# q's and k's high parts kept once in DRAM, and each stack loaded in two transfers

## The chip, the core and the metric

The kernel runs on one core of a Trainium2 chip. A core has TensorE (PE: matmuls, with its weight loads shown apart as PEld), VectorE (DVE), ScalarE (ACT), GpSimd (POOL) and SyncE (SP), each with its own queue of instructions that it takes in order, and 16 DMA engines that move data between DRAM and the core's SBUF. The metric is the time of one execution in microseconds on the device, the median of several runs. The profile is of one further execution.

## The reference

The kernel computes, for x of 2048 rows and 512 columns, a gated mix of a sliding-window attention and a dense block. All matmuls are asked in float32.

```python
x = A_x
g = _sigmoid((x * gate_w).sum(-1, keepdims=True))
a = _A_ref(x, A_wqkv, A_wo)              # 32 heads of 16, window of 256 keys, softmax
b = _B_ref(x, B_w1, B_b1, B_w2, B_b2)    # 512 -> 1792, gelu, -> 512
return g * a + (1 - g) * b
```

In `_A_ref` the scores are q·k / 4 per head, masked to keys at most 255 places back, then softmax, then times v, then the output projection.

## The kernel before

**Precision by two parts.** A float32 number is kept as a high part (rounded to the matmul's type) and a low part (the rest). A product is then made of three: high·high, high·low and low·high. For the projections this is three matmuls (`mm3`, L101 to L103). For the scores, where a head has only 16 numbers, the three products are stacked along the contraction: 48 rows hold 16 dimensions times three parts. q's rows carry low, high, high, k's rows high, low, high.

**Stages.** First `qkv` computes q, k and v for four pieces of 512 rows (t = 0 to 3). `qk_out` splits each 128 x 512 result into its parts in the tile `qke` and stores them to the DRAM tiles `SQ[t]` and `SK[t]`, in which the rows of a head lie by dimension and part: 8 heads of a column group, 16 dimensions, 3 parts, 4 column groups, 512 positions. The store is two transfers: L327 writes both parts, L328 writes the high part once more as the third.

Then attention runs over 8 groups of four heads and, in each, over 16 blocks of 128 keys: 128 blocks in all. Four blocks, one piece of 512 positions, make what is called a stretch here; there are 32. Every block has four matmuls `sm` (L517), whose row maxima DVE takes, and, 12 blocks later in the order, four matmuls `st` (L563), of which ACT takes the exponential. The products with v (`pv`, L607) come once for each stretch, behind the first three st of the next. `sm` reads the stacks `qd` (48 rows for each of two heads, 96 together) and `kd`; `st` reads the stacks `qs` and `ks`, which have 4 more rows for the maxima. In between the matmuls of attention the dense block's matmuls (`u`, `y`) are dealt out, so that TensorE always has one at hand.

**The loads around the change.** All transfers are issued by SP, from one queue, in the order in which the program wrote them. `kd`, `qd` and `ks` have two slots, one for the stretch at work and one for the next. When the maxima of a stretch begin, `load_kd` (L486) and `load_qd` (through `put_pairs`, L478 for one head's rows, L473 and L475 for the other's) are written for the next one; when its st begin, `load_ks` (the same three lines of `put_pairs`). `load_qs` (L497, two transfers) is written about three stretches ahead. `kd` takes two transfers where the window reaches back into the piece before, otherwise one. In the same queue stand the loads of the dense block's weights (`raw_w`, L163, which ACT then copies at L171), its input (`mx`, L676), its partial sums (`YA`, `YB`, `ya`), v (`vbuf`, L503), and the normalization of the attention: numerator and denominator out (`ND`, L635), the denominator back (`den`, L645, whose reciprocal DVE takes at L649), its reciprocal out and back, broadcast (`RD` L652, `rb` L657), the product out (`OT`, L664). The program places the readers of such a load a fixed time behind it in their engines' queues; an engine that gets there early waits.

**What an SP instruction waits for.** Beside its data's semaphores every transfer carries one of eight completion semaphores, DMAHW0 to DMAHW7, called lanes here. They are dealt out in turn, and a transfer is issued only when the one before it on its lane has landed. So at most eight transfers are on their way.

Of the kernel before, what the change touches and what calls it, by code (L numbers as in the profile page):

```python
# [9 lines left out]
F32 = mybir.dt.float32  # L10
# [7 lines left out]
S, D, F, H, DH, W = 2048, 512, 1792, 32, 16, 256  # L18
T = 512
NT = S // T  # L20
NB = T // 128
NC = D // 128
# [10 lines left out]
def gated_mix(ctx: ExitStack, tc: tile.TileContext, x, wqkv, wo, w1, b1, w2, b2, gate_w, out):  # L33
    nc = tc.nc
    x = x[0]
# [4 lines left out]
    dr = ctx.enter_context(tc.tile_pool(name="dr", bufs=1, space=DRAM))  # L40
# [4 lines left out]
    def f32(ap):  # L45
        return ap.bitcast(F32)
# [2 lines left out]
    nc.gpsimd.memset(idle, 0.0)  # L49


    SQ = [dr.tile([H // NC, 16, 3, NC, T], F32, name=f"SQ{t}") for t in range(NT)]
    SK = [dr.tile([H // NC, 16, 3, NC, T], F32, name=f"SK{t}") for t in range(NT)]
    SV = [dr.tile([128, NB, 2, H // 2 * 17], F32, name=f"SV{t}") for t in range(NT)]
    XT = [dr.tile([NC, 128, 2, T], F32, name=f"XT{t}") for t in range(NT)]
    OT = [dr.tile([NC, 128, T], F32, name=f"OT{t}") for t in range(NT)]
# [20 lines left out]
    for r in (0, 64):  # L77
        for e in (0, 1):
            v = cut[r:r + 64, e]
# [7 lines left out]
    for s in (0, 1):  # L87
        for k in (0, 1):
            v = own[64 * s:64 * s + 4].rearrange("r (p s) -> r s p", s=2)[:, s]
# [18 lines left out]
    def after(ns, fn, *args):  # L108
        now[1] += 1
        heapq.heappush(todo, (now[0] + ns, now[1], fn, args))  # L110

    def step_todo():
        due, _, fn, args = heapq.heappop(todo)
        keep, now[0] = now[0], due
        fn(*args)
        now[0] = max(keep, due)
# [6 lines left out]
    def need(*keys):  # L123
        for key in keys:
            while key not in done:
                step_todo()
# [88 lines left out]
    qs = cp.tile([128, 2, S], F32R, name="qs")  # L215
    ks = cp.tile([128, 2, 2, 2 * T], F32R, name="ks")
    qd = cp.tile([128, 2, 2, 2 * T], F32R, name="qd")
    kd = cp.tile([128, 2, 2, W + T], F32R, name="kd")
# [93 lines left out]
    def qk_out(t, j, p):  # L312

        dst, i = (SQ[t], j) if j < NC else (SK[t], j - NC)
        e = sb.tile([128, 2, T], F32R, tag="h", bufs=7, name=f"qke{t}_{j}")

        h = 1 if j < NC else 0

        def hi():
            nc.scalar.activation(e[:, h], p, AF.Copy)  # L320

        def lo():
            nc.vector.tensor_sub(e[:, 1 - h], p, f32(e[:, h]))  # L323

        def store():
            to = dst[:, :, :, i].rearrange("h d s c -> (h d) s c")
            nc.sync.dma_start(to[:, 0:2], f32(e))  # L327
            nc.sync.dma_start(to[:, 2], f32(e[:, h]))  # L328
            done.add(("qk", t, j))
        after(100, hi), after(700, lo), after(700 + HOLDQ, store)  # L330

# [36 lines left out]
    def qkv(t):  # L368
# [30 lines left out]
        for n, (kind, j) in enumerate(pieces):  # L399
# [18 lines left out]
            if t == 2 and n in (1, 2):  # L418
                load_kd(0, n - 1)
            if t == 2 and n in (8, 9):  # L420
                load_ks(0, n - 8)
# [22 lines left out]
    def slot(g_, c):  # L444
        return (g_ * NT + c) % 2

    def heads(st, g_):

        return st[2 * (g_ % 4):2 * (g_ % 4) + 2, :, :, 2 * (g_ // 4):2 * (g_ // 4) + 2]

    def ready(t, g_, k):
        need(*[("qk", t, k * NC + 2 * (g_ // 4) + a) for a in range(2)])

    def part(st, g_, s):

        return heads(st, g_)[s].rearrange("d u a c -> (d u) (a c)")

    def load_ks(g_, c):


        ready(c, g_, 1)
        n = 2 * NB
        put_pairs([f32(ks[64 * s + 4:64 * s + 52, slot(g_, c)]) for s in range(2)], SK[c], g_)

    def put_pairs(to, st, g_):

        n = 2 * NB
        for s in range(2):
            v = to[s].rearrange("r a x -> r (a x)")
            src = part(st, g_, s)  # L470
            if s:
                mid = v[:, 192:192 + 256 * (n - 1)].rearrange("r (n x) -> r n x", x=256)[:, :, 0:128]
                nc.sync.dma_start(mid, src[:, 64:64 + 128 * (n - 1)].rearrange("r (n x) -> r n x", x=128))  # L473
                ends = v.rearrange("r (n j) -> r n j", j=64)[:, 0:4 * n:4 * n - 1]
                nc.sync.dma_start(ends, src.rearrange("r (n j) -> r n j", j=64)[:, 0:2 * n:2 * n - 1])  # L475
            else:
                v = v.rearrange("r (n x) -> r n x", x=256)[:, :, 64:192]
                nc.sync.dma_start(v, src.rearrange("r (n x) -> r n x", x=128))  # L478

    def load_kd(g_, c):  # L480
        for t in range(max(c - 1, 0), c + 1):
            ready(t, g_, 1)
            k0 = 0 if t == c else T - W
            at = W if t == c else 0
            src = heads(SK[t], g_)[:, :, :, :, k0:].rearrange("s d u a c -> (s d u) a c")
            nc.sync.dma_start(f32(kd[0:96, slot(g_, c), :, at:at + T - k0]), src)  # L486

    def load_qd(g_, c):
        ready(c, g_, 0)
        put_pairs([f32(qd[48 * s:48 * s + 48, slot(g_, c)]) for s in range(2)], SQ[c], g_)  # L490

    def load_qs(g_, c):
        ready(c, g_, 0)
        need(("v", NT - 2, NB - 1))
        for s in range(2):
            v = f32(qs[64 * s + 4:64 * s + 52, :, c * T:(c + 1) * T])
            nc.sync.dma_start(v, part(SQ[c], g_, s).rearrange("r (a c) -> r a c", a=2))  # L497

    def att_load_v(g_, c):
        need(*[("v", c, b) for b in range(NB)])  # L500
# [171 lines left out]
    def load_x(t, name):  # L672
        xt = sb.tile([128, NC, 2, T], F32R, tag="xt", bufs=1, name=f"{name}{t}")

        def part(c):
            nc.sync.dma_start(f32(xt[:, c]), XT[t][c])  # L676
            if c == NC - 1:
                done.add(name)
        for c in range(NC):
            after(MXAT * c, part, c)  # L680
        xts[t] = xt
# [235 lines left out]
    for c in (0, 1):  # L917
        load_qd(0, c)
    fill(AHEAD)
    for u in range(-LEAD, NU):  # L920
        m = u + LEAD
        gm, bm = divmod(m, NKB)
        step = STEP if u >= 0 else STEP0
        for i in range(4):
            if i == 1 and m % NB == 0 and NB <= m < NU - NB:
                load_kd(*divmod(m // NB + 1, NT)), load_qd(*divmod(m // NB + 1, NT))
            for op in ORDER:
                if op == "s" and u >= 0:
                    att_exp(u // NKB, u % NKB, i)
                if op == "m" and m < NU:  # L930
                    att_max(gm, bm, i ^ XOR)
                if op == "p" and i == PVAT and u >= 1:
                    att_pvs(u - 1)
                if op == "f":
                    fill(step / 4 / ORDER.count("f"))
        if m < NU and bm % RB == RB - 1:
            after(900, att_rows, gm, bm // RB)
        if m % NB == QAT % NB and QAT <= m < QAT + NKB:
            load_qs(0, (m - QAT) // NB)
        if u % NB == 0 and NB <= u < NU - NB:  # L940
            load_ks(*divmod(u // NB + 1, NT))
        if u % NB == 2 and NB < u < NU - 3 * NB:
            load_qs(*divmod(u // NB + 3, NT))
        if u % NB == 0 and u >= 0:
            att_load_v(*divmod(u // NB, NT))
        if u - NU + NKB in (9, 11, 13):
            load_y((u % NKB - 9) // 2)
# [60 lines left out]
```

## Time and profile before

| | |
|---|---|
| median of 3 runs | 758.23 us (756.12 to 759.04) |
| the profiled execution | 755.15 us, its span 753.4 us |
| granted TensorE clock | 0.998 |
| DMA | 172.10 MB, mean 228 GB/s |
| HBM | read 108.53 MB, written 62.39 MB |
| chain that ended last | PE 83%, DMA 6%, DVE 4%, ACT 3% |

The profile names engines as above; SPq is SP's queue of DMA issues, L12 is line 12 of the kernel, and `out<-in` are the program's own names of the tiles. Times are in microseconds from the start of the span where nothing else is said. The time of an SPq row is that of the issue, not of the transfer. A wait row tells who waited, for whom, the sum, how often, and the longest.

### The profile page before, as it was taken

To read this page: it belongs to the slowest core of one execution; us is meant where nothing else is said; L and a number is where in the kernel's file an instruction comes from. 1 tells how busy PE (TensorE), PEld (TensorE's weight loads), DVE (VectorE), ACT (ScalarE), POOL (GpSimd) and SP (SyncE) were. 2 spreads that over 40 slices of the span, in tenths; PEclk is the share of its full clock that TensorE was granted. 3 is DMA by queue.
4 is the path that set the end of the run, shared out by engine and by line. 5 is a ranking of instruction groups with operands and counts; after the bars stand their busy time and mean duration, and the time that the engine had idled before them with its cause. 6 is when DMAs were issued, how large, how long until landed. Compare 5 with 4: busy or idle time off the path is not lost.

```text
span 753.4 us, 17968 instructions
## 1 busy us (share of the span) xinstructions
PE 737.4 (98%) x6129; PEld 608.8 (81%) x6129; DVE 519.2 (69%) x1567; ACT 431.4 (57%) x972; POOL 373.0 (50%) x846
## 2 busy tenths in 40 slices
PE   8999999989999999999999999999999999999998
PEld 7888888877888888888887877888888888878787
DVE  4522325779767866986798699768867886784562
ACT  4434532348646844864696478547845864785541
POOL 4200000338866765785677567757865875630000
PEclk9999999999999999999999999999999999999999
DMA  9879899998999699799986899998799999638683
GB/s 296 335 242 398 276 390 262 245 324 172 265 233 203 139 229 220 180 212 227 205 186 158 219 218 205 263 248 160 174 233 246 180 215 273 152 88 260 211 271 123
DMA packets 179258, 172.10 MB, mean 228 GB/s; under 512 B 56672, under 2 KB 122976, under 8 KB 179168
## 3 DMA queue, kind: packets, MB, share of 16 engines
q1 hardware_dynamic: 179168, 170.97, 87.6%
q8 instruction: 48, 0.79, 0.5%
q14 instruction: 42, 0.34, 0.2%
HBM read 108.53 MB, written 62.39 MB: 227 GB/s over the span
## 4 chain that ended last, share of the span: by engine, by line
PE 83%; DMA 6%; DVE 4%; ACT 3%; issue 2%; SPq 1%; POOL 1%; DVEq 0%; ACTq 0%; POOLq 0%
PE sm L517 9%; PE st L563 8%; PE pv_sm L607 7%; PE y L101 7%; PE y L103 6%; PE y L102 6%; PE u L101 5%; PE u L103 5%; PE u L102 5%; PE qk L103 4%; PE qk L101 4%; PE qk L102 4%; PE v L103 2%; PE v L102 2%; PE v L101 2%
## 5 line engine op out<-in xcount | busy, mean ns | idle before, releaser
L522 DVE CUSTOM_DVE_ANT_0 jm<-sm,mask 128x320 bf16<-128x320 f32 (+4 forms) x512 | 237.8, 464 | 81.1 <-PE sm L517 54.4
L579 POOL TENSOR_SCALAR_AFFINE_SELECT pt<-pt 64x256 f32<-64x256 f32 (+1 forms) x538 | 226.6, 441 | 115.0 <-ACT pt L585 104.4
L585 ACT ACTIVATE pt<-st 128x320 f32<-128x320 f32 (+4 forms) x512 | 206.9, 425 | 131.4 <-PE st L563 128.5
L517 PE MATMUL sm<-kd,qd 96*128 96x320 f32 (+4 forms) x512 | 157.7, 311 | 5.9 <-DVE M L522 4.5
L563 PE MATMUL st<-qs,ks 128*128 128x320 f32 (+4 forms) x512 | 155.7, 308 | 1.0 <-ACT pt L585 0.9
L545 POOL CAST qs<-tt 4x256 fp32r<-4x256 f32 x256 | 126.4, 494 | 44.3 <-DVE tt L538 33.4
L517 PEld LDWEIGHTS sm<-kd,qd 96*128 96x128 f32 x512 | 96.4, 188 | 31.1 <-DVE M L522 9.5
L563 PEld LDWEIGHTS st<-qs,ks 128*128 128x128 f32 x512 | 98.1, 192 | 22.2 <-ACT pt L585 3.1
L101 PE MATMUL y<-w,h 128*128 128x512 f32 x224 | 90.1, 402 | 0.0
L103 PE MATMUL y<-w,h 128*128 128x512 f32 x224 | 88.8, 396 | 0.3 <-DVE h L736 0.2
L102 PE MATMUL y<-w,h 128*128 128x512 f32 x224 | 87.7, 392 | 0.0
L101 PE MATMUL u<-mx,w 128*128 128x512 f32 x196 | 80.1, 409 | 0.0
L103 PE MATMUL u<-mx,w 128*128 128x512 f32 x196 | 77.5, 395 | 0.0
L102 PE MATMUL u<-mx,w 128*128 128x512 f32 x196 | 76.9, 392 | 0.0
L607 PE MATMUL pv_st<-pt,vbuf 64*32 64x320 f32 (+4 forms) x1408 | 73.3, 346 | 2.5 <-DVE pt L573 1.3
L607 PE MATMUL pv_sm<-pt,vbuf 64*32 64x320 f32 (+4 forms) x1408 | 74.2, 346 | 0.3 <-POOL pt L579 0.3
L607 PEld LDWEIGHTS pv_sm<-pt,vbuf 64*32 64x32 f32 x1408 | 51.1, 106 | 19.3 <-issue 2.5
L323 DVE TENSOR_TENSOR qke<-qk,qke 128x512 fp32r<-128x512 f32 x32 | 22.1, 691 | 48.5 <-ACT qke L320 38.0
L103 PEld LDWEIGHTS y<-w,h 128*128 128x128 f32 x224 | 42.1, 188 | 10.9 <-DVE h L736 1.1
L320 ACT ACTIVATE qke<-qk 128x512 fp32r<-128x512 f32 x32 | 19.1, 598 | 55.3 <-PE qk L103 35.6
L607 PEld LDWEIGHTS pv_st<-pt,vbuf 64*32 64x32 f32 x1408 | 46.2, 106 | 2.8 <-DVE pt L573 1.5
L336 POOL MEMSET vx<- 128x32 f32 x16 | 2.4, 156 | 92.0 <-DMA SK<-qke 28.8
(148 smaller groups left out, 1338.7 us busy)
## 6 DMA issues: line engine op xcount, KB each, us to landing
kd<-SK SPq DMA_DIRECT2D x32, 384.0 KB
qs<-SQ SPq DMA_DIRECT2D x64, 192.0 KB
mx<-XT SPq DMA_DIRECT2D x24, 512.0 KB
SQ<-qke SPq DMA_DIRECT2D x16, 512.0 KB
SK<-qke SPq DMA_DIRECT2D x16, 512.0 KB
ND<-nd SPq DMA_DIRECT2D x32, 256.0 KB
raw_w<-in_B_w_dram SPq DMA_DIRECT2D x28, 256.0 KB
ks<-SK SPq DMA_DIRECT2D x32, 192.0 KB
```

Source lines behind the costliest of these rows:

```text
L101: nc.tensor.matmul(p, lh, rh, start=first, stop=False)
L102: nc.tensor.matmul(p, lh, rl, start=False, stop=False)
L103: nc.tensor.matmul(p, ll, rh, start=False, stop=last)
L320: nc.scalar.activation(e[:, h], p, AF.Copy)
L323: nc.vector.tensor_sub(e[:, 1 - h], p, f32(e[:, h]))
L517: nc.tensor.matmul(p[:, :w], qd[0:96, n, pr, 128 * j:128 * (j + 1)], kd[0:96, n, pr, k1 - w:k1], start=True, stop=True)
L522: nc.vector.tensor_tensor_reduce(junk[:, :w], p[:, :w], mask[:, 320 - w:320], 1.0, -3e38, ALU.add, ALU.max, M[:, 2 * (b % RB) + hb, pr:pr ...
L545: nc.gpsimd.tensor_copy(dst, src.unsqueeze(1).broadcast_to([4, 2, RB, 32]))
L563: nc.tensor.matmul(p[:, :w], ks[:, slot(g_, kb // NB), pr, at:at + 128], qs[:, pr, k0:k0 + w], start=True, stop=True)
L579: nc.gpsimd.affine_select(out=v, in_=v, pattern=[[0, v.shape[1]], [1 - 2 * e, 64]], compare_op=ALU.is_ge, fill=0.0, base=-e, channel_multi ...
L585: nc.scalar.activation(pt[:, hf, pr, :w], p[:, :w], AF.Exp, scale=SCALE)
L607: nc.tensor.matmul(pv[r // 64][32 * i:32 * i + 32, q - c * T:e - c * T], vts[g_, b // NB][r:r + 64, v:v + 32], rhs(r), start=start, stop=s ...
```

## The change

DRAM now holds two parts of q and k for each dimension, not three, and a store is one transfer of 512 KB. The stacks in SBUF still have 48 rows a head. They are filled by two transfers where there was one: the first brings the 32 rows of both parts, the second the 16 rows that repeat the high part, read again from the same place in DRAM. The rows of a stack are reordered for this: `ks`, `qs` have the 32 rows of a head first and then its 16; `kd`, `qd` the 32 rows of both heads and then the 16 of both. q and k are reordered alike, so the sum over the rows is the same.

```diff
-    SQ = [dr.tile([H // NC, 16, 3, NC, T], F32, name=f"SQ{t}") for t in range(NT)]
-    SK = [dr.tile([H // NC, 16, 3, NC, T], F32, name=f"SK{t}") for t in range(NT)]
+    SQ = [dr.tile([H // NC, 16, 2, NC, T], F32, name=f"SQ{t}") for t in range(NT)]
+    SK = [dr.tile([H // NC, 16, 2, NC, T], F32, name=f"SK{t}") for t in range(NT)]
...
         def store():
-            to = dst[:, :, :, i].rearrange("h d s c -> (h d) s c")
-            nc.sync.dma_start(to[:, 0:2], f32(e))
-            nc.sync.dma_start(to[:, 2], f32(e[:, h]))
+            nc.sync.dma_start(dst[:, :, :, i].rearrange("h d s c -> (h d) s c"), f32(e))
             done.add(("qk", t, j))
...
+    HI = {"q": slice(1, 2), "k": slice(0, 1)}
+
+    def put_parts(put, rows, st, g_, s, kind):
+
+        for v, u in zip(rows, (slice(0, 2), HI[kind])):
+            put(v, heads(st, g_)[s, :, u].rearrange("d u a c -> (d u) (a c)"))
+
+    def rows_of(v, s):
+
+        return v[64 * s + 4:64 * s + 36], v[64 * s + 36:64 * s + 52]
...
-        put_pairs([f32(ks[64 * s + 4:64 * s + 52, slot(g_, c)]) for s in range(2)], SK[c], g_)
+        v = f32(ks[:, slot(g_, c)])
+        put_pairs([rows_of(v, s) for s in range(2)], SK[c], g_, "k")
...
+        for s in range(2):
+            put_parts(put, to[s], st, g_, s, kind)
 
     def load_kd(g_, c):
...
-            src = heads(SK[t], g_)[:, :, :, :, k0:].rearrange("s d u a c -> (s d u) a c")
-            nc.sync.dma_start(f32(kd[0:96, slot(g_, c), :, at:at + T - k0]), src)
+            to = f32(kd[0:96, slot(g_, c), :, at:at + T - k0])
+            src = heads(SK[t], g_)[:, :, :, :, k0:]
+            nc.sync.dma_start(to[0:64], src.rearrange("s d u a c -> (s d u) a c"))
+            nc.sync.dma_start(to[64:96], src[:, :, 0].rearrange("s d a c -> (s d) a c"))
...
-        put_pairs([f32(qd[48 * s:48 * s + 48, slot(g_, c)]) for s in range(2)], SQ[c], g_)
+        v = f32(qd[0:96, slot(g_, c)])
+        put_pairs([(v[32 * s:32 * s + 32], v[64 + 16 * s:80 + 16 * s]) for s in range(2)], SQ[c], g_, "q")
...
         for s in range(2):
-            v = f32(qs[64 * s + 4:64 * s + 52, :, c * T:(c + 1) * T])
-            nc.sync.dma_start(v, part(SQ[c], g_, s).rearrange("r (a c) -> r a c", a=2))
+            put_parts(put, rows_of(f32(qs[:, :, c * T:(c + 1) * T]), s), SQ[c], g_, s, "q")
```

The instructions of PE, DVE, ACT and POOL keep their order; only SP's queue changes. Its first stores, before (the lane that an issue waits for stands in brackets; names end in the buffer's number, and the number behind DMAHW says only which lane):

```order
L327 DMA SQ_70<-qke_0_297 128x2x512 [waits DMAHW1_49,DVE_49]
L328 DMA SQ_70<-qke_0_297 128x512 [waits DMAHW2_49]
L327 DMA SK_74<-qke_4_312 128x2x512 [waits DMAHW3_49,DVE_49]
L328 DMA SK_74<-qke_4_312 128x512 [waits DMAHW4_49]
L401 DMA XT_82<-ks 128x1024 [waits DMAHW5_49]
```

and now:

```order
L326 DMA SQ_70<-qke_0_297 256x1x512 [waits DMAHW1_49,DVE_49]
L326 DMA SK_74<-qke_4_312 256x1x512 [waits DMAHW2_49,DVE_49]
L399 DMA XT_82<-ks 128x1024 [waits DMAHW3_49]
L243 DMA xr_0_345<-in_A_x_dram 128x512 [waits DMAHW4_49,DVE_49,PE_49]
L243 DMA xr_1_347<-in_A_x_dram 128x512 [waits DMAHW5_49,DVE_49,PE_49]
```

Each second store is gone, and what follows it moves up by one place and one lane.

SP's queue where one stretch's kd and qd and then the next ks are issued (this is the stretch whose kd goes out at 454.90 us in the profile), before:

```order
L486 DMA kd<-SK_74 96x2x256 [waits DMAHW5_49,PE_49]
L486 DMA kd<-SK_75 96x2x512 [waits PE_49]
L478 DMA qd<-SQ_71 48x8x128 [waits DMAHW7_49]
L473 DMA qd<-SQ_71 48x7x128 [waits DMAHW0_49]
L475 DMA qd<-SQ_71 48x2x64 [waits DMAHW1_49]
L163 DMA raw_w_6578<-in_B_w_dram 128x512 [waits DMAHW2_49,DVE_49]
L478 DMA ks<-SK_76 48x8x128 [waits DMAHW3_49,PE_49]
L473 DMA ks<-SK_76 48x7x128 [waits DMAHW4_49]
L475 DMA ks<-SK_76 48x2x64 [waits DMAHW5_49]
```

and now, from the second kd to the first ks:

```order
L494 DMA kd<-SK_75 64x2x512 [waits DMAHW0_49,PE_49]
L495 DMA kd<-SK_75 32x2x512 [waits DMAHW1_49]
L483 DMA qd<-SQ_71 32x8x128 [waits DMAHW2_49]
L483 DMA qd<-SQ_71 16x8x128 [waits DMAHW3_49]
L478 DMA qd<-SQ_71 32x7x128 [waits DMAHW4_49]
L480 DMA qd<-SQ_71 32x2x64 [waits DMAHW5_49]
L478 DMA qd<-SQ_71 16x7x128 [waits DMAHW6_49]
L480 DMA qd<-SQ_71 16x2x64 [waits DMAHW7_49]
L163 DMA raw_w_6744<-in_B_w_dram 128x512 [waits DMAHW0_49,DVE_49]
L483 DMA ks<-SK_76 32x8x128 [waits DMAHW1_49,PE_49]
```

followed by

```order
L483 DMA ks<-SK_76 16x8x128 [waits DMAHW2_49]
L478 DMA ks<-SK_76 32x7x128 [waits DMAHW3_49]
L480 DMA ks<-SK_76 32x2x64 [waits DMAHW4_49]
L478 DMA ks<-SK_76 16x7x128 [waits DMAHW5_49]
L480 DMA ks<-SK_76 16x2x64 [waits DMAHW6_49]
L515 DMA vbuf<-SV_79 128x8x34 [waits DMAHW7_49]
```

Nine transfers from the first kd to the last ks have become 17, and the weights in their midst (`raw_w`) stand eleventh where they stood sixth.

More of the change, by code (lines that the diff above doesn't have):

```diff
@@ L452, in ready, with put_pairs, put @@
         need(*[("qk", t, k * NC + 2 * (g_ // 4) + a) for a in range(2)])
-    def part(st, g_, s):
-        return heads(st, g_)[s].rearrange("d u a c -> (d u) (a c)")
+    HI = {"q": slice(1, 2), "k": slice(0, 1)}
[4 more added lines that the diff above has]
+        return v[64 * s + 4:64 * s + 36], v[64 * s + 36:64 * s + 52]
     def load_ks(g_, c):
         ready(c, g_, 1)
+        v = f32(ks[:, slot(g_, c)])
+        put_pairs([rows_of(v, s) for s in range(2)], SK[c], g_, "k")
+    def put_pairs(to, st, g_, kind):
         n = 2 * NB
-        put_pairs([f32(ks[64 * s + 4:64 * s + 52, slot(g_, c)]) for s in range(2)], SK[c], g_)
[L465 to L470, printed above, removed]
+        def put(rows, src):
+            v = rows.rearrange("r a x -> r (a x)")
             if s:
@@ L494, in load_qs, with put @@
         need(("v", NT - 2, NB - 1))
+        def put(rows, src):
+            nc.sync.dma_start(rows, src.rearrange("r (a c) -> r a c", a=2))
         for s in range(2):
-            v = f32(qs[64 * s + 4:64 * s + 52, :, c * T:(c + 1) * T])
-            nc.sync.dma_start(v, part(SQ[c], g_, s).rearrange("r (a c) -> r a c", a=2))
+            put_parts(put, rows_of(f32(qs[:, :, c * T:(c + 1) * T]), s), SQ[c], g_, s, "q")
     def att_load_v(g_, c):
```

## The prediction, made before the changed kernel ran

> **What bounds the kernel now.** I read the page's busy times first, then the windows by stage, then the SP queue's timeline, and last the distance from a load's issue to its first reader.
>
> ```profile
> span 753.4 us, 17968 instructions
> PE 737.4 (98%) x6129; PEld 608.8 (81%) x6129; DVE 519.2 (69%) x1567; ACT 431.4 (57%) x972; POOL 373.0 (50%) x846
> q1 hardware_dynamic: 179168, 170.97, 87.6%
> ...
> 90.00:120.00 30.00, 30.00 (x140) 24.42 (x139) 9.09 (x18) 8.78 (x27) 0.78 (x5) 1.00 1.00 342
> 120.00:150.00 30.00, 30.00 (x144) 25.38 (x143) 20.49 (x81) 9.63 (x28) 7.60 (x14) 1.00 0.94 268
> 150.00:180.00 30.00, 27.65 (x126) 22.70 (x125) 24.84 (x76) 18.08 (x36) 13.98 (x24) 0.94 1.03 270
> 180.00:210.00 30.00, 28.36 (x286) 22.57 (x286) 25.10 (x81) 19.81 (x45) 25.20 (x55) 1.00 0.90 231
> ```
>
> A window's columns are its length, busy time (count) of PE, PEld, DVE, ACT and POOL, granted clock, DMA share and GB/s. TensorE is the bound: it idles for 753.4 - 737.4 = 16.0 us in all, and not at all from 90 to 150 us, where q and k are being stored. A lighter DMA load can win only where PE idles beside DMA work, above all the 2.35 + 1.64 = 4.0 us of 150 to 210 us. What the change can lose is cover: the DMA engines are busy for 87.6% of the span, and every transfer goes through SP's one queue.
>
> **What it removes.** The 32 second stores at L328, 16 of q and 16 of k.
>
> ```profile
> L328 SPq DMA_DIRECT2D SQ<-qke x16: 447/932/1214, 14.4 to 158.4; - x16
> L328 SPq DMA_DIRECT2D SK<-qke x16: 327/1013/1290, 15.9 to 163.3; - x16
> ```
>
> The three numbers are the least, median and greatest ns of one issue, then come the first and last start. That is 16 x 0.93 + 16 x 1.01 = 31 us of SP and 32 x 256 KB = 8.4 MB of the 171 MB, all before 164 us. Nearly all of it lies under a TensorE without a gap, so I take it at nothing; without that cover it would be worth what PE idles there, not 31 us.
>
> **What it adds.** Every stack's load is cut in two by rows: bytes and rows stay, the transfers grow in number. Before:
>
> ```profile
> L486 SPq DMA_DIRECT2D kd<-SK x56: 304/398/1789, 85.6 to 624.5; - x56
> L497 SPq DMA_DIRECT2D qs<-SQ x64: 322/435/1517, 147.4 to 649.9; - x64
> L478 SPq DMA_DIRECT2D ks<-SK x32: 303/376/1509, 108.7 to 680.0; - x32
> L473 SPq DMA_DIRECT2D ks<-SK x32: 302/470/1270, 109.9 to 680.4; - x32
> L475 SPq DMA_DIRECT2D ks<-SK x32: 302/462/1084, 110.7 to 680.9; - x32
> ```
>
> Added are 56 of kd, 64 of qs, 96 of ks, and 96 of qd, which goes through the same three lines: 312 against the 32 removed. What does one cost? By the shapes in the order, L475 moves 48 x 2 x 64 numbers of 4 bytes, 24 KB, and takes 0.46 us to issue; L473 moves 48 x 7 x 128, 168 KB, and takes 0.47: the price goes by the transfer, not by its bytes. So SP gets 312 x 0.46 = 144 us more work, over about 600 us. SP computes nothing; this costs time only where a load then lands after its reader wants it.
>
> The Trainium skill speaks against the change here: "DMA: Bandwidth & Descriptors", section "Rules for kernel authors", says that small transfers should be joined, those under 64 KB being mostly overhead, and that one transfer is better than two to disjoint partition halves. The equal issue times of L473 and L475 agree with the first. The same page, section "Anatomy of one DMA", gives a fixed part of about 2.0 us for each, taken on another issuing path; as an estimate the 280 more transfers would by that fill 280 x 2.0 / 8 = 70 us on each of the eight lanes, which only matters if the lanes are already full.
>
> **How the queue stands in a stretch.** A stretch is four key blocks; 32 of them run between the first st and the last, (702.2 - 163.6) / 32 = 16.8 us each. In each, SP issues kd and qd and then ks for the next stretch, so these have most of a stretch to land. A calm stretch and a crowded one:
>
> ```profile
> L563 PE MATMUL st<-qs,ks x512: 193/309/468, 163.6 to 702.2; 128*128 128x320 f32 x149, 128*128 128x256 f32 x6, 128*128 128x64 f32 x6, 128*128 128x128 f32 x5
> ...
> 301.55 0.46 SPq L475 DMA_DIRECT2D qd<-SQ  x1
> 305.65 0.34 SPq L664 DMA_DIRECT2D OT<-num  x1
> 306.09 0.58 SPq L478 DMA_DIRECT2D ks<-SK  x1
> ...
> 454.90 0.89 SPq L486 DMA_DIRECT2D kd<-SK  x2
> ...
> 456.84 0.30 SPq L473 DMA_DIRECT2D qd<-SQ  x1
> 457.73 0.30 SPq L475 DMA_DIRECT2D qd<-SQ  x1
> 458.68 0.35 SPq L163 DMA_DIRECT2D raw_w<-in_B_w_dram  x1
> 459.65 0.30 SPq L478 DMA_DIRECT2D ks<-SK  x1
> 460.66 0.31 SPq L475 DMA_DIRECT2D ks<-SK  x1
> ```
>
> Columns: start, time of the issue. In the calm stretch SP is free from 302.0 to 305.65, so the added kd and qd transfers (about four, 1.9 us) vanish in that hole, and ks is late only by its own three, 1.4 us. In the crowded one the rows from 456.84 on are about 0.95 us apart although an issue takes 0.30: as the order shows, the two qd rows wait for a lane alone, that is for the landing of an earlier transfer, and the weights and ks for a lane too. There nothing is free. From kd to the last ks, before, nine transfers take 460.97 - 454.90 = 6.1 us; after, there are 17. How long the 17 take no row shows, so I bound it. From below: if only the issues count, 17 x 0.46 = 7.8 us, 1.7 us later, since the bytes that the lanes wait for are the same. From above: if each transfer keeps its pace of 6.1 / 9 = 0.67 us, 11.5 us, 5.4 us later. I take 2.4 us, near the lower end, because most of the added transfers carry a third of the bytes or less.
>
> **Where that meets TensorE.** The ks stack is the one with little to spare. A stretch's first st stands against the last issue of its ks so:
>
> ```profile
> 212.23 0.30 SPq L475 DMA_DIRECT2D ks<-SK  x1
> L563 PE MATMUL st<-qs,ks x3: 305/309/383, 217.9 to 220.0; 128*128 128x320 f32 x3
> ...
> 680.95 0.55 SPq L475 DMA_DIRECT2D ks<-SK  x1
> L563 PE MATMUL st<-qs,ks x3: 304/306/308, 688.1 to 689.7; 128*128 128x320 f32 x3
> ...
> 164.43 6.60 DMA qs<-SQ
> 455.34 5.56 DMA kd<-SK
> 656.33 1.83 DMA raw_wo<-in_A_wo_dram
> ```
>
> The second kind of row is the group of three st that opens a stretch. From issue to first use it is 217.9 - 212.2 = 5.7 us in the tightest stretch and 7.1 us in the one near 688; read so, nine of the 30 stretches from 200 us on lie under 8.3 us (5.7, 6.4, 6.7, 6.9, 7.1, 7.9, 8.0, 8.2, 8.3), the others at 9.3 and above. The last three rows, of the chain, show what a transfer takes from its issue to its landing: 5.6 to 6.6 us for a stack's, say 6.1, and 1.8 us for one of 64 KB in a quiet queue. The slack of the nine is then 0, 0.3, 0.6, 0.8, 1.0, 1.8, 1.9, 2.1 and 2.2 us. A lateness of 2.4 us leaves TensorE waiting 2.4 + 2.1 + 1.8 + 1.6 + 1.4 + 0.6 + 0.5 + 0.3 + 0.2 = 10.9 us. With 1.7 us it would be 5.8, with 5.4 us 37.9. The waiting st stands ahead of everything else on PE, so these waits are paid in full.
>
> Behind SP's queue there are also the weight loads and the denominators, for which ACT and DVE wait in order:
>
> ```profile
> ACT w L171 <- DMA raw_w<-in_B_w_dram: 7.3, 5, 2.1
> DVE den L649 <- DMA den<-ND: 6.1, 6, 1.9
> ```
>
> Of 28 and 16, 5 and 6 wait now. If those 11 wait 2.4 us longer, ACT and DVE lose 26 us; both have idle time, and PE waits only when their PSUM buffers run out. Bounds: nothing, or all 26. I take 2 us, nearer to nothing: 13.4 us of such waits stand beside only 16.0 us of PE's idle time from every cause.
>
> From 150 to 210 us the kernel has fewer store bytes and more transfers. At best the 4.0 us of idle time go, at worst kd and qd are late there too, by one 2.4 us. I take 0.
>
> **Sum**: 10.9 + 2 + 0 = 12.9 us on the profiled execution's 755.2 us, 768.1 us. The median of the three runs shown, 758.2, lies 3.1 us above that execution, so 771 us.
>
> **Rivals.** (1) The lanes become the bound: a transfer keeps its pace of 0.67 us however small. Every crowded stretch then ends when its ks lands: 37.9 us, with the 2 us 40, so 798 us. For it: the 0.95 us, the same from row to row. Against it: those lanes were waiting for a 384 KB kd and weights.
> (2) Absorbed: the last ks transfers, of 8 and 56 KB now, find fewer bytes queued ahead and land sooner after their issue. Halfway between 6.1 and the 1.8 us of the small transfer is 4.0, and those 2.1 us pay for the 2.4. What is left is the 2 us and some tenths, 758 to 761 us, no change. For it: the same bytes pass the same engines. Against it: the crowded stretch's SP has no free time.
> (3) Faster: the stores were the disturbance. Without them the SP queue and the DMA engines, at a share of 1.03 from 150 to 180 us, reach the attention unclogged; the idle 4.0 us go, and with the clock's dip to 0.94 (6% of 30 us) another 1.8: 752 us. It decides if all added loads after 210 us stay within their slack. Against it: the nine stretches above.
> That the change doesn't do what it says I leave out: the order shows 32 stores gone and every load doubled.
>
> **Numbers.** Late ks, as forecast: 0.58, by itself 763 to 785 us. Rival 1: 0.12; rival 2: 0.18; rival 3: 0.12. Range 756 to 791 us: it takes in rival 2 and reaches toward rival 1. A difference of 0.5%, 3.8 us, is about what can be told from none. Faster by more: 0.12; within: 0.20; slower: 0.68.
>
> **What would show it.** Right: waits of PE st L563 for ks transfers in the changed kernel's waits, 1 to 4 us each, in the stretches near 218, 351, 624 and 672 us; the SP queue nearly without holes there; PE's busy time unchanged, its idle time near 29 us; before 120 us the same times, with a lower DMA share. Wrong: PE's idle time at 16 us, which is rival 2; idle time mostly before DVE's and ACT's results instead of at st, which would make the second term the main one; or a loss spread over all 32 stretches, which is rival 1.

## The result and the profile after

The changed kernel takes 786.4 us (median of 6 runs, 783.9 to 787.1), the kernel before 758.6 us (756.1 to 760.6) on the same chip: a ratio of 1.037, 95% interval 1.034 to 1.040, 27.8 us more. The forecast was slower, 771 us, in a range that ended at 791. The direction was right; of the amount, 12.9 us were forecast, less than half. Among the experiments' runs below, one of a_whole and one of b_tiny_pool fell in a slower state of the chip (granted clock 0.85 and 0.70) and are left out of the times given.

The page of the changed kernel, busy times, DMA queue and the two groups of attention matmuls (busy time and mean ns, then the idle time before them and what ended most of it):

```profile
span 785.4 us, 18285 instructions
PE 747.1 (95%) x6129; PEld 611.2 (78%) x6129; DVE 518.8 (66%) x1567; ACT 431.1 (55%) x972; POOL 369.1 (47%) x846
q1 hardware_dynamic: 179552, 162.60, 76.0%
...
L529 PE MATMUL sm<-kd,qd 96*128 96x320 f32 (+4 forms) x512 | 159.6, 315 | 13.5 <-DVE nd L643 8.9
L575 PE MATMUL st<-qs,ks 128*128 128x320 f32 (+4 forms) x512 | 157.6, 311 | 15.1 <-DMA ks<-SK 8.8
```

The span grew by 785.4 - 753.4 = 32.0 us. TensorE's idle time went from 16.0 to 785.4 - 747.1 = 38.3 us, 22.3 more; 14.1 of these stand before st (15.1 against 1.0) and 7.6 before sm (13.5 against 5.9). The other 9.7 us are busy time: the same 6129 matmuls took 747.1 us, not 737.4. The DMA engines have become freer, 76% against 87.6%, so it is not their load that grew.

Who TensorE waited for (sum, times, longest):

```profile
PE sm L529 <- DVE nd L643: 8.9, 5, 4.9
PE st L575 <- DMA ks<-SK: 8.8, 4, 3.4
PE st L575 <- ACT pt L597: 6.4, 7, 2.2
```

Before, and in the page's groups the idle time before sm and st:

```profile
PE sm L517 <- DVE nd L631: 1.0, 1, 1.0
...
L517 PE MATMUL sm<-kd,qd 96*128 96x320 f32 (+4 forms) x512 | 157.7, 311 | 5.9 <-DVE M L522 4.5
L563 PE MATMUL st<-qs,ks 128*128 128x320 f32 (+4 forms) x512 | 155.7, 308 | 1.0 <-ACT pt L585 0.9
```

No st waited for ks then. Of the three rows above, the second was forecast; the other two fall to the prediction's second term, which had 2 us. So of TensorE's new idle time 8.8 us end with a ks, but 7.9 + 5.5 = 13.4 us with a result of DVE or ACT.

sm waits for `nd` because in the program the products with v and sm take turns on the same three PSUM buffers, and `nd` is the copy that frees one of them. `nd` stands in DVE's queue, and in the longest case this is why it was late, in the chain of waits, in DVE's waits and in TensorE's timeline:

```profile
468.86 7.56 DMA den<-ND
476.51 0.36 DVE den L661
479.17 0.61 DVE nd L643
...
DVE den L661 <- DMA den<-ND: 15.3, 9, 4.4
...
479.82 0.53 PE L529 MATMUL sm<-kd,qd 96*128 96x192 f32 x1 [4.90 <-DVE nd L643]
```

DVE reaches the reciprocal of a denominator that has not landed, waits in order, and everything behind it waits too. Its waits for den went from 6.1 us in 6 cases to 15.3 us in 9, and one of them left TensorE idle for 4.9 us. ACT does the same with a late weight: it waits 2.56 us for it, the next exponential comes late, and st, which waits for that, stands idle for 2.21 us:

```profile
461.07 0.63 ACT L171 ACTIVATE w<-raw_w 128x512 fp32r<-128x512 f32 x1 [2.56 <-DMA raw_w<-in_B_w_dram]
```

And the granted clock. Windows set on what the trace shows of it (the last three columns are clock, DMA share and GB/s):

```profile
356.90:363.70 6.80, 5.43 (x51) 4.17 (x59) 1.94 (x7) 1.31 (x3) 0.58 (x2) 0.50 1.06 304
462.70:466.10 3.40, 3.40 (x12) 2.85 (x11) 3.26 (x10) 2.94 (x8) 1.91 (x4) 0.51 0.84 164
479.80:483.20 3.40, 3.38 (x11) 2.99 (x12) 2.28 (x12) 2.49 (x6) 0.00 (x0) 0.50 0.70 179
653.90:657.30 3.40, 3.40 (x48) 2.53 (x54) 1.00 (x4) 0.87 (x2) 0.11 (x1) 0.50 1.06 322
```

Each begins in, or about 1 us or less behind, one of TensorE's four longest gaps (3.2, 2.2, 4.9 and 3.4 us). TensorE is busy at half the clock for 5.43 + 3.40 + 3.38 + 3.40 = 15.6 us, half of which, 7.8 us, is lost. Before, there was one such window, at a gap of 2.0 us that ends at 166.95 us:

```profile
166.70:170.10 3.40, 3.15 (x9) 2.76 (x10) 3.12 (x13) 1.82 (x5) 1.15 (x2) 0.50 1.08 296
```

That one costs 1.6 us, so 7.8 - 1.6 = 6.2 of the 9.7 us of busy time are the clock's; the other 3.5 I did not trace. The Trainium skill, "TensorE: Matmul & The Clock Gate", section "Why this matters for your kernels", warns of gaps above some 3 us. Here gaps of 2.0 and 2.2 us were enough. The length of a gap alone does not decide: in a_den_late, below, gaps of 2.31 us (to 218.66 us) and 2.85 us (to 358.22 us) were followed by the full clock, and one of 1.63 us (to 493.17 us) by half of it.

### The profile page after: what moved, and what is told of

It reads as the page before. It is cut to its first block, busy times and chain, and to the rows that moved or that the text cites. A ratio compares the mean times of both kernels' runs of the same rounds, so it can differ in the third digit from the quotient of the medians.

```text
span 785.4 us, 18285 instructions
## 1 busy us (share of the span) xinstructions
PE 747.1 (95%) x6129; PEld 611.2 (78%) x6129; DVE 518.8 (66%) x1567; ACT 431.1 (55%) x972; POOL 369.1 (47%) x846
## 4 chain that ended last, share of the span: by engine, by line
PE 70%; DMA 14%; DVE 6%; issue 3%; ACT 3%; SPq 3%; POOL 0%; DVEq 0%; ACTq 0%; POOLq 0%
PE sm L529 7%; PE st L575 6%; PE pv_sm L619 5%; PE u L101 5%; PE y L101 5%; PE u L103 4%; PE u L102 4%; PE y L103 4%; PE y L102 4%; PE qk L103 4%; PE qk L101 4%; PE qk L102 4%; DMA den<-ND 2%; DMA ks<-SK 2%; DMA kd<-SK 2%
## 5 line engine op out<-in xcount | busy, mean ns | idle before, releaser
L591 POOL TENSOR_SCALAR_AFFINE_SELECT pt<-pt 64x256 f32<-64x256 f32 (+1 forms) x538 | 223.9, 436 | 147.6 <-ACT pt L597 137.7
L529 PE MATMUL sm<-kd,qd 96*128 96x320 f32 (+4 forms) x512 | 159.6, 315 | 13.5 <-DVE nd L643 8.9
L575 PE MATMUL st<-qs,ks 128*128 128x320 f32 (+4 forms) x512 | 157.6, 311 | 15.1 <-DMA ks<-SK 8.8
L575 PEld LDWEIGHTS st<-qs,ks 128*128 128x128 f32 x512 | 99.0, 193 | 37.8 <-issue 10.7
L102 PE MATMUL u<-mx,w 128*128 128x512 f32 x196 | 77.6, 396 | 0.0
L619 PEld LDWEIGHTS pv_sm<-pt,vbuf 64*32 64x32 f32 x1408 | 51.0, 108 | 20.6 <-issue 3.2
L736 DVE SCALAR_TENSOR_TENSOR sqh<-sqh,x1h 128x512 f32<-128x512 f32 x56 | 41.8, 747 | 12.3 <-ACT sqh L733 12.1
```

Source lines behind the costliest of these rows:

```text
L102: nc.tensor.matmul(p, lh, rl, start=False, stop=False)
L529: nc.tensor.matmul(p[:, :w], qd[0:96, n, pr, 128 * j:128 * (j + 1)], kd[0:96, n, pr, k1 - w:k1], start=True, stop=True)
L575: nc.tensor.matmul(p[:, :w], ks[:, slot(g_, kb // NB), pr, at:at + 128], qs[:, pr, k0:k0 + w], start=True, stop=True)
L591: nc.gpsimd.affine_select(out=v, in_=v, pattern=[[0, v.shape[1]], [1 - 2 * e, 64]], compare_op=ALU.is_ge, fill=0.0, base=-e, channel_multi ...
L619: nc.tensor.matmul(pv[r // 64][32 * i:32 * i + 32, q - c * T:e - c * T], vts[g_, b // NB][r:r + 64, v:v + 32], rhs(r), start=start, stop=s ...
L736: nc.vector.scalar_tensor_tensor(sq, sq, GC, x1, op0=ALU.add, op1=ALU.mult)
```

## The experiments

All are timed against the kernel before on the same chip; the brackets hold the 95% interval of the ratio. The kernel before has medians of 756.9 to 758.6 us in these comparisons, so a difference between experiments on different chips is uncertain by up to 2 us.

**Number of transfers, layout or stores?** a_whole: the changed kernel's DRAM and store, every stack loaded whole.

```diff
+        flat = st.rearrange("h d u a c -> (h d u) a c")
+        return flat[r:r + 48 * heads_, 2 * (g_ // 4):2 * (g_ // 4) + 2]
...
-        put_pairs([rows_of(v, s) for s in range(2)], SK[c], g_, "k")
+        put_pairs([v[64 * s + 4:64 * s + 52] for s in range(2)], SK[c], g_, "k", True)
```

> The changed kernel with its stores and its two parts in DRAM, but every stack loaded whole again, 48 rows in one transfer: the last 16 rows of a stack are then the next head's rows in DRAM and not the repeated high part, so the scores are other numbers, from as many bytes and rows. Theory 'count' (the loss comes from 312 more transfers in SP's queue): back at the time of the kernel before, 756 to 760 us, TensorE idle for about 16 us. Theory 'layout' (the loss comes from how the two parts lie in DRAM and are read): stays above 775 us. Rival 'stores' of the prediction (the removed stores were a disturbance): 752 us.

756.8 us, ratio 1.000 [0.997, 1.004]. With as many transfers a load as before, nothing is lost: DRAM's new layout and the single store cost nothing, and win nothing either.

a_stores_back:

```diff
             nc.sync.dma_start(dst[:, :, :, i].rearrange("h d s c -> (h d) s c"), f32(e))
+            nc.sync.dma_start(SX[t][j], f32(e[:, h]))
```

> The changed kernel, and each qke's high part stored once more, 256 KB, into a DRAM tile that nothing reads: the 32 removed transfers are back, and nothing else differs. Theory 'count': the stores lie under a TensorE that never waits there, so 786 to 789 us, as the changed kernel, at most 3 us more. If the removed stores gave back a real gain that the loads then ate, it shows here: 792 us or more.

795.5 us, 1.053 [1.048, 1.058]: 9 us above the changed kernel (10.7 when each is taken against the kernel before on its own chip), a miss for "at most 3". The stores that win nothing with whole loads win 9 us with split ones. The window of 90 to 180 us shows where, first in the changed kernel:

```profile
90.00:180.00 90.00, 88.10 (x413) 72.09 (x411) 56.04 (x177) 37.62 (x93) 23.90 (x45) 1.00 0.84 248
```

and in a_stores_back:

```profile
90.00:180.00 90.00, 81.44 (x371) 66.06 (x370) 47.65 (x153) 28.98 (x75) 14.21 (x31) 0.98 0.86 273
```

TensorE does 6.7 us less there. The first of its new waits is 2.5 us of sm for a late qd; three of 1.8 to 2.1 us for DVE's maxima follow, whose origin I did not trace. So the change has a cost of 37 us or a little more and a relief of some 10, of which the result shows the difference.

b_tiny: the kernel before, with a transfer of 64 bytes behind each load of a stack.

```diff
+    def more():
+        k = tiny[0] % 8
+        tiny[0] += 1
+        nc.sync.dma_start(scr[:, k:k + 1], b1[0:16].unsqueeze(1))
...
                 nc.sync.dma_start(v, src.rearrange("r (n x) -> r n x", x=128))
+                more()
```

> The kernel before, and behind each of its loads of a stack one more transfer of 16 numbers (64 bytes in all) into a small tile that nothing reads: 280 + 32 = 312 more transfers at the places where the change adds them, with no bytes, no cut and the layout of before. Theory 'count': 775 to 790 us, most of the loss of the change, with late ks and den as there. Theory 'layout', or one by which the cut of the rows itself is what costs: 758 to 764 us.

795.0 us, 1.052 [1.047, 1.056], above the range. It is the time of a_stores_back, the kernel with the same stores and as many transfers, to 0.5 us. So neither the cut of the rows nor their bytes are needed for the loss: 312 more transfers in SP's queue, almost without bytes, cost as much. SP's issue of one takes 0.45 us here (median). This run does not part the issues in SP's queue from the lanes that the transfers occupy.

b_tiny_pool issues those from GpSimd instead.

```diff
-        nc.sync.dma_start(scr[:, k:k + 1], b1[0:16].unsqueeze(1))
+        nc.gpsimd.dma_start(scr[:, k:k + 1], b1[0:16].unsqueeze(1))
```

> b_tiny with its 312 tiny transfers issued from GpSimd's queue instead of SP's: as many transfers on the same DMA engines, none of them in SP's queue nor on its eight lanes. Theory 'queue': 756 to 766 us, if GpSimd, which is idle half of the time, can take them. If the number of transfers on the DMA engines is what costs: 790 us, as b_tiny.

788.8 us, 1.040 [1.036, 1.045], which looks like the rival's number. TensorE's waits say what it is:

```profile
PE pv_st L621 <- POOL pt L593: 10.8, 6, 2.2
PE sm L531 <- DVE M L536: 4.7, 8, 2.1
...
L101 POOL DMA_DIRECT2D scr<-in_B_b_dram x312: 487/487/648, 71.2 to 698.6; - x156
```

No st waits for ks, and sm for nd only once. Instead GpSimd, 0.49 us busy with each issue, comes late with its own work on `pt`. The price has moved to another queue, so the run does not tell what the transfers cost the DMA engines; they are not shown to cost anything there, nor to be free.

**Which of the loads?** Each of these splits one part and loads the rest whole, as in a_whole.

> As a_whole (two parts in DRAM, one store, kd, qd and qs loaded whole, with the next head's rows as their last 16), but ks in two transfers a piece as in the changed kernel: 96 more transfers. Theory 'slack' of the prediction (ks is the stack with little to spare, its own lateness is the loss): 768 us or more, with waits of st for ks. Theory 'queue' (SP's queue has holes that take up some transfers, the loss comes when all of them are filled, whichever load fills them): 757 to 765 us, and the three kernels with one part split lose less together than the 28 us of the change.

766.9 us, 1.012 [1.008, 1.016].

> As a_whole, but kd and qd in two transfers a piece as in the changed kernel: 152 more transfers, which stand ahead of ks in the queue. Theory 'slack': kd and qd have 6 us and more to spare, so only what they delay counts: 762 to 770 us. Theory 'queue': 760 to 770 us, more than ks or qs alone since they are more transfers.

762.5 us, 1.006 [1.004, 1.009].

> As a_whole, but qs in two transfers a piece as in the changed kernel: 64 more transfers, whose readers come some 30 us later. Theory 'slack': no change against a_whole, 756 to 759 us, as they stand behind ks in each stretch. Theory 'queue': 757 to 763 us, the least of the three.

758.8 us, 1.002 [0.999, 1.005]. Against their common 757.3 us that is 9.6, 5.2 and 1.5 us (the last within its interval), together 16.3: what is lost together is more. 766.9 lies between the ranges of "slack" and "queue", and the waits are not those that "slack" named. TensorE's and DVE's waits in a_only_ks:

```profile
PE sm L538 <- DVE nd L652: 6.6, 3, 4.4
PE st L584 <- DMA ks<-SK: 0.5, 1, 0.5
...
DVE den L670 <- DMA den<-ND: 10.9, 6, 3.7
```

st waits for ks hardly at all; sm waits behind denominators that had come late. Whether they are what the time is lost to, ks_den_late below tells.

**The denominators.** a_den_late gives them time:

```diff
-DIVS = ((6000, 9000, 12000, 21500, 23500), (4500, 5700, 8500, 17000, 18500))
+DIVS = ((9000, 12000, 15000, 24500, 26500), (4500, 5700, 8500, 17000, 18500))
```

> The changed kernel, with the reciprocal of a denominator and all that follows it placed 3 us later in the order for the first three quarters of the normalizations; as many transfers. If DVE's wait for den, in order, is what makes sm wait (the 8.9 us of sm behind DVE nd and part of the clock's dips), this brings back 5 to 12 us: 774 to 781 us, with DVE's waits for den under 6 us. If DVE's waits are covered by its idle time, as the prediction had it: 785 to 788 us.

775.8 us, 1.022 [1.017, 1.026]: 10.6 us come back with as many transfers as before. What is left at the head of TensorE's waits:

```profile
PE st L575 <- DMA ks<-SK: 9.3, 4, 3.7
PE sm L529 <- DVE M L534: 6.3, 11, 1.4
```

The waits for nd are gone, those for ks are whole. Is the move good by itself?

> The kernel before with the reciprocal and what follows 3 us later: what that move is worth without the change. DVE waits there for den 6.1 us in all and sm for nd 1.0 us: 755 to 759 us, no change. If the move is worth as much here as in the changed kernel (10 us), a_den_late says nothing on the added transfers.

755.2 us, 0.996 [0.994, 0.998]: 3.2 us better than the kernel before, and the best kernel of this study. So of the 10.6 us some 7.4 belong to the change. In b_den_late's profile sm waits for DVE's maxima 2.3 us and st never for ks.

> a_only_ks (only ks in two transfers, the other stacks whole) with the reciprocal of the denominators and what follows 3 us later, as in a_den_late. If a_only_ks loses its 9.6 us because den lands late behind 3 more transfers, so that DVE, then sm, then the clock wait (4.4 us of gap at 465 us and 6.8 us at half the clock): 756 to 760 us. If it loses them because ks itself is late: 764 us or more.

763.2 us, 1.008 [1.005, 1.011], between the two expectations: 3.7 us of the 9.6 go with the denominators (about what the move is worth anyway), 8.0 above b_den_late stay. So the denominators were not the price of these 96 transfers. With den out of the way ks itself is late, and the wait has only changed its name:

```profile
PE sm L538 <- DVE M L543: 4.4, 10, 1.0
PE st L584 <- DMA ks<-SK: 3.3, 3, 1.5
```

**Is what is left ks's own?** The next two start from a_den_late and load one stack whole.

> a_den_late with ks loaded whole (its last 16 rows are the next head's, other scores): 216 instead of 312 more transfers. Theory 'slack': ks's lateness is most of what is left, 757 to 764 us. Theory 'queue': in proportion to the transfers, some 6 us of the 20 come back, 767 to 772 us; if it is the crossing of a limit that counts, 757 to 764 us here too, and then den_qs_whole decides.

762.4 us, 1.007 [1.005, 1.010]: 13.4 of the 20.6 us between a_den_late and b_den_late.

> a_den_late with qs loaded whole (likewise): 248 instead of 312 more transfers, the 64 that have 30 us to spare themselves and stand ahead of kd, qd and ks of the next step. Theory 'slack': they cost nothing, 774 to 777 us. Theory 'queue': a load with time to spare costs as much as any, since what stands behind it is late: 762 to 771 us.

775.3 us, 1.022 [1.018, 1.026]: nothing. 64 transfers fewer in the same queue change nothing when they are those of a load with time to spare. "Slack" was right and "queue" wrong. The place of ks in its stretch says the same. Over the 30 stretches from 200 us on, its last issue, counted from the first st of the stretch in which it is issued, is later than in the kernel before by a median of 5.1 us in the changed kernel, 2.6 in a_only_ks, 2.3 in a_only_kdqd, 0.0 in a_only_qs and 4.9 in den_qs_whole. What makes ks late are its own transfers and those of kd and qd, and the two add up.

**Another order.** a_ks_first:

```diff
+            if i == 1 and u % NB == 0 and NB <= u < NU - NB:
+                load_ks(*divmod(u // NB + 1, NT))
             if i == 1 and m % NB == 0 and NB <= m < NU - NB:
                 load_kd(*divmod(m // NB + 1, NT)), load_qd(*divmod(m // NB + 1, NT))
```

> The changed kernel with the load of ks written ahead of kd and qd of the same step (it is released by then) instead of some 3 us of program behind them: as many transfers, other places in the queue. Theory 'count', by which 15 us of TensorE's new waits stand at st for ks, and the clock's dips behind them cost more: 765 to 778 us, no wait of st for ks over 1 us, kd and qd a little later without a wait. If the late denominators are the larger part: 780 us or more.

796.2 us, 1.053 [1.049, 1.057], 10 us worse. (The expectation's 15 us are all of the idle time before st; 8.8 of them were waits for ks.) st no longer waits for ks, but other waits grew by more: st's for ACT from 6.4 to 11.2 us, sm's for `nd` from 8.9 to 10.2, and qd itself is late.

```profile
PE st L575 <- ACT pt L597: 11.2, 10, 4.2
PE sm L529 <- DVE nd L643: 10.2, 6, 3.9
...
PE sm L529 <- DMA qd<-SQ: 2.4, 2, 2.1
```

> The changed kernel with both: ks ahead of kd and qd in the queue, and the reciprocal 3 us later. a_ks_first alone lost 10 us more, a_den_late alone won 10. If ks's lateness (9.3 us of st waits in a_den_late) can be bought with the slack of kd and qd once den is out of the way: 765 to 772 us. If the queue has too much in it for any order: 778 us or more.

792.2 us, 1.047 [1.042, 1.052], the second of the two expectations: in this order the lateness of ks cannot be paid with the slack of kd and qd. It is not ks or den any more. No st waits for ks, and DVE waits for den 2.5 us; but other small loads of the same queue are late:

```profile
PE sm L529 <- DVE M L534: 16.3, 16, 3.5
ACT w L171 <- DMA raw_w<-in_B_w_dram: 20.0, 11, 4.8
```

ACT's waits for the weights were 10.0 us in the changed kernel. Behind two of sm's longest waits for the maxima, those that end at 353.09 and 600.14 us, the chain leads through DVE to the landing of an `rb` and of a `YB`.

## Why the prediction was right in direction and too small

**The bound and the stores.** That the stores lie under a busy TensorE is what a_whole shows, with whole loads. The third piece, "from 150 to 210 us I take 0", was right as a sum (TensorE is busy for 88.1 us from 90 to 180 us, 87.7 before) but not as reasoned: with the stores back the added transfers would have cost some 10 us more, most of it before 180 us.

**The price of one transfer** was 0.46 us for each, by the transfer and not by its bytes. Now, for the smallest transfers (8 and 16 KB) and for the first of kd's:

```profile
L480 SPq DMA_DIRECT2D ks<-SK x64: 302/431/1435, 107.5 to 712.4; - x64
L494 SPq DMA_DIRECT2D kd<-SK x56: 573/601/1443, 85.4 to 658.0; - x56
```

0.43 us, as taken; b_tiny shows the same with 64 bytes. kd went from 0.40 to 0.60, a smaller miss.

**The lateness.** I had the calm stretch absorb kd's and qd's transfers in a hole of the queue, so that ks would be 1.4 us late. The same stretch now:

```profile
300.37 0.62 SPq L669 DMA_DIRECT2D rb<-RD  x1
301.08 0.40 SPq L824 DMA_DIRECT2D YA<-yo  x1
301.54 3.77 SPq L507 DMA_DIRECT2D qs<-SQ  x4
305.36 0.59 SPq L657 DMA_DIRECT2D den<-ND  x1
306.05 0.61 SPq L494 DMA_DIRECT2D kd<-SK  x1
306.70 0.59 SPq L495 DMA_DIRECT2D kd<-SK  x1
307.33 1.88 SPq L483 DMA_DIRECT2D qd<-SQ  x2
309.26 0.43 SPq L478 DMA_DIRECT2D qd<-SQ  x1
309.73 0.44 SPq L480 DMA_DIRECT2D qd<-SQ  x1
...
311.79 0.91 SPq L483 DMA_DIRECT2D ks<-SK  x2
...
314.17 0.43 SPq L480 DMA_DIRECT2D ks<-SK  x1
```

There is no hole. SP issues from end to end, and the last ks is issued 12.6 us after the stretch's first st (which runs at 301.5), not 6.3 us after it (307.3 against 301.0): 6.3 us late, not 1.4. Here kd itself goes out 5.3 us later in its stretch, behind qs and den, and the way from it to the last ks grew only from 7.1 to 8.1 us. Two of the issues are long, one of qs with 2.36 us and one of qd with 1.39; why is not shown. The median of the 30 stretches is 5.1 us, near the prediction's upper bound of 5.4 and twice the 2.4 that it took. What qs adds ahead of kd is not the reason: with qs whole, in den_qs_whole, the last ks is as late.

The landing was off the other way. The prediction's 6.1 us came from a qs and a kd; a ks transfer now lands in 3.9 and 4.2 us in the two tightest cases of the chain:

```profile
213.39 3.85 DMA ks<-SK
353.98 4.20 DMA ks<-SK
```

If the last completion update on a transfer's lane before the lane is used again is read as its landing, the smallest transfers of ks landed after 5.8 us before (L475, median from 200 to 700 us) and land after 3.0 us now (L480). In b_tiny those of L475, with bytes and shape unchanged, land after 2.9 us, so their size is not the reason.

The two errors are of opposite sign and about equal, so it is luck that the waits of st for ks came out at 8.8 us (9.3 in a_den_late) where 10.9 were forecast. They stand in four stretches, not nine. (The upper bound of 37.9 us was itself too low: with 5.4 us some of the stretches at 9.3 us and above, which it leaves out, wait too.)

**The steps that failed** are the prices of lateness in the two terms. The larger miss is in the first, "so these waits are paid in full": it counted st's own waits and nothing that follows from them. The waits came as forecast, but a_den_late, in which den has time, is 20.6 us above b_den_late, nearly twice the 10.9 us of the term. The profiles of the two, a_den_late first, show where the time goes:

```profile
span 777.7 us, 18272 instructions
PE 745.3 (96%) x6129; PEld 608.9 (78%) x6129; DVE 517.9 (67%) x1567; ACT 430.7 (55%) x972; POOL 371.6 (48%) x846
...
span 752.3 us, 17950 instructions
PE 736.8 (98%) x6129; PEld 606.3 (81%) x6129; DVE 517.7 (69%) x1567; ACT 430.7 (57%) x972; POOL 373.1 (50%) x846
...
PE sm L517 <- DVE M L522: 2.3, 6, 0.8
```

The span differs by 25.4 us (this execution of a_den_late was its longest). 9.3 us are st's waits for ks. Another 7.6 us are idle time for which the sum had no term; sm's waits for DVE's maxima, 6.3 us against 2.3, are the largest part. And 8.5 us are busy time: two windows at half the clock, 3.4 us each, make 3.4 of them. What lengthens the other 5.1 us, and why the maxima come late, stays open.

The second is "I take 2 us, nearer to nothing" for weights and denominators. a_den_late against b_den_late puts the denominators at some 7 us of the 27.8. Read as above, they landed no sooner than before (median 5.0 us, 4.7 before), unlike ks, so nothing made up for SP's lateness. The prediction argued from the 16.0 us of idle time of the kernel before that little of such waits reaches TensorE; the 4.9 us of sm behind one late denominator show that more does when the wait is longer. How the 7 us and the 20.6 us split between causes depends on the order in which they are removed: in a_only_ks the same move of den wins only 0.5 us more than in the kernel before.

**The rivals.** That the lanes set the pace is not what the trace shows: in the stretch above SP's rows stand end to end, all but two issues at 0.4 to 0.6 us, the pace of issuing, and SP's waits for a landing, summed over all its lines, fell from 128 to 95 us with 280 more transfers. "Absorbed" was right that ks lands sooner, by more than it said, but not that this pays for all; it holds for the 64 transfers of qs alone (1.002). "Faster" is refuted by a_whole. Of what I named as proof, PE's st waits came in three of the four stretches, those near 218, 351 and 624 us before, and a fourth came where none was named (at 509 us now); the times before 120 us stayed, with a DMA share of 0.83 against 1.00 from 90 us on; the idle time was 38 us, not 29, and PE's busy time did not stay unchanged. The sign against it, idle time mostly before DVE's and ACT's results, came too (13.4 of the 22.3 us). Yet the second term is not the main one: with den out of the way 20.6 of the 27.8 us stay.

## What to carry to other kernels

A load cut in two costs by its transfers, not by its bytes: count the issues between the moment at which a buffer comes free and the load's last transfer. Transfers of a load with time to spare, as qs here, cost nothing beside them. Look at every load that shares the queue, the small ones with a reader in an in-order engine first: the denominators here, 16 KB each, cost some 7 us. Price a wait of the bounding engine at more than its length: here 9.3 us of waits came with a loss of 20.6. And the name of the longest wait is not yet its cause: when the denominators got time, or ks its place, the wait moved to the next late load in the queue.

## What the runs showed of the hardware that was not expected

The granted clock went to half for 3.4 or 6.8 us at gaps of TensorE of 2.2 us and more, four times in the changed kernel, and in a_den_late at one of 1.6 us but not at those of 2.31 and 2.85 us. The smallest transfers of ks landed sooner, after 3.0 us instead of 5.8, also with the same bytes and shape (2.9 us in b_tiny), while the DMA engines' share of the span fell from 87.6% to 76.0% (77.6% in b_tiny); that the one is the reason for the other is not shown. An issue from GpSimd took 0.49 us of that engine for 64 bytes.
